# A banded convolution turned round: taps as the stationary operand on 96-token tiles of two token streams, and a transposing DMA to bring the result to channels

## Chip, cores and metric

One core of a Trainium2 chip. The metric is device time in microseconds (us); most executions of one kernel lie within 0.3% of each other. The kernel before takes 400.06 us (median of 3 runs, 399.44 to 400.3).

## The reference, cut to what matters

```python
# x: (8, 4224, 192); weight: (8 heads, 7 taps); w_in: (192, 2*512); A_log: (512,); w_out: (512, 192)
w = softmax(weight, axis=-1)                         # per head, 24 channels a head
xc[b, s, h, g] = sum_k w[h, k] * x[b, s - 6 + k, h, g]    # causal, zeros before each sequence
val, gate = split(xc @ w_in)
h_t = exp(A_log) * h_{t-1} + val_t                   # along each sequence, per inner channel
out = (silu(gate) * h) @ w_out
```

## The kernel before

A step is 1024 tokens of one of the four blocks of 128 inner channels; four steps make a period, 33 periods the loop. The convolution multiplies x (stationary, that is loaded as weights: 128 tokens x 32 padded channels of a head) by a band of taps (moving, that is streamed past them: 134 columns). So its result already has channels on the partitions, as the projections want it. PSUM is the memory that TensorE writes its results to; an eviction is the copy out of it.

```python
ps_c = ctx.enter_context(tc.tile_pool(name="ps_c", bufs=1, space=bass.MemoryType.PSUM))
ps_v = ctx.enter_context(tc.tile_pool(name="ps_v", bufs=2, space=bass.MemoryType.PSUM))
# ... taps: VectorE builds fz, ScalarE's queue writes it to memory and reads the band back
nc.scalar.dma_start(fa, fz.rearrange("p h f -> p (h f)"))
nc.scalar.dma_start(
    tb, dataclasses.replace(fa, offset=FL, ap=[[H * FR - 1, P], [FR, H], [1, W]])
)
# ...
def conv(p):                       # 512 tokens
    pc = ps_c.tile([P, 2, N], FP32, name="pc")
    for b in range(NB):
        for h in range(H):
            q = C32 * (h % HG)
            nc.tensor.matmul(pc[q : q + C32, h // HG, b * P : b * P + w],
                             xb[:, b, h, :], tb[:, h, 0:w], ...)
        # ... at the first block, 8 matmuls of 6 columns for the tokens of the tile before
    nc.scalar.copy(xc, pc)
# ...
def scan(s):                       # one scan of 1024 tokens, cut where a sequence starts
    for lo, hi in zip(ends, ends[1:]):
        nc.vector.tensor_tensor_scan(h[:, lo:hi], av[...], pv[:, lo:hi],
                                     initial=0.0 if lo in cuts else last[c], ...)
# ... loop, per step: scan, gate, output projection of six steps ago,
#     a convolution in every second step, val of the next step, gate, product on GpSimd
```

Of the kernel before, what the change touches and what calls it, by code (L numbers as in the profile page):

```python
# [37 lines left out]
def kernel(  # L38
# [22 lines left out]
    NP = T // N  # L61
    NS = T // N2
    BPB = S // P
    NC = DI // P
    HG = H // 2
    C32 = 32
    assert NS * N2 == T and BPB * P == S and NC == 4 and G <= C32 and HG == 4
    W = P + HALO
    FL = P - 1
# [3 lines left out]
    x4 = xf.rearrange("(n b p) d -> n p b d", b=NB, p=P)  # L73
# [6 lines left out]
    xc_pool = ctx.enter_context(tc.tile_pool(name="xc", bufs=5))  # L80
# [8 lines left out]
    XB = 4  # L89
    raw = {}  # L90

    def load(p):
        t = xraw_pool.tile([P, NB, D], FP32, name="xraw")
        nc.sync.dma_start(t, x4[p])
        raw[p] = t


    FR = FL + W
    ws = singles.tile([P, H, KW], FP32, name="ws")
    nc.sync.dma_start(  # L100
        ws, dataclasses.replace(weight, ap=[[0, P], [KW, H], [1, KW]])
    )
    load(0)
    load(1)


    win = singles.tile([P, 2, D2], BF16, name="win")
    for h in range(H - 1):
        nc.gpsimd.dma_start(  # L109
            win[C32 * (h % HG) : C32 * (h % HG) + C32, h // HG, :],  # L110
            moe_w_in[h * G : h * G + C32, :],
        )
    nc.gpsimd.dma_start(win[96 : 96 + G, 1, :], moe_w_in[(H - 1) * G : H * G, :])
    nc.gpsimd.dma_start(win[96 + G : P, 1, :], moe_w_in[0 : C32 - G, :])  # L114
    xbs = []
    for j in range(XB):
        xb = singles.tile([P, NB, H, C32], BF16, name=f"xb_{j}")
        nc.gpsimd.memset(xb[:, :, :, G:C32], 0.0)
        xbs.append(xb)

    fz = singles.tile([P, H, FR], BF16, name="fz")
# [3 lines left out]
    wmax = singles.tile([P, H], FP32, name="wmax")  # L125
    nc.vector.tensor_reduce(wmax, ws, axis=mybir.AxisListType.X, op=Alu.max)
    nc.vector.tensor_tensor(  # L127
        ws, ws, wmax.unsqueeze(2).to_broadcast([P, H, KW]), op=Alu.subtract
    )
    nc.scalar.activation(ws, ws, Act.Exp)  # L130
    wsum = singles.tile([P, H], FP32, name="wsum")
    nc.vector.tensor_reduce(wsum, ws, axis=mybir.AxisListType.X, op=Alu.add)
    winv = singles.tile([P, H], FP32, name="winv")
    nc.vector.reciprocal(winv, wsum)
    for k in range(KW):
        nc.vector.tensor_tensor(  # L136
            fz[:, :, FL + HALO - k], ws[:, :, k], winv, op=Alu.mult
        )
    f_dram = nc.dram_tensor("taps_scratch", (P, H * FR), BF16, kind="Internal")
    fa = f_dram.ap()  # L140
    nc.scalar.dma_start(fa, fz.rearrange("p h f -> p (h f)"))
    tb = singles.tile([P, H, W], BF16, name="tb")
    nc.scalar.dma_start(
        tb, dataclasses.replace(fa, offset=FL, ap=[[H * FR - 1, P], [FR, H], [1, W]])
# [6 lines left out]
    def cast(p):  # L151
        nc.gpsimd.tensor_copy(  # L152
            xbs[p % XB][:, :, :, 0:G],
            raw.pop(p).rearrange("p b (h g) -> p b h g", g=G),
        )

    cast(0)
    cast(1)
    wout = singles.tile([P, NC, D], BF16, name="wout")
    nc.gpsimd.dma_start(wout, moe_w_out.rearrange("(c p) m -> p c m", p=P))  # L160
    for p in range(2, 6):
        load(p)
    cast(2)
    cast(3)

    xcs = {}

    def conv(p):
        pc = ps_c.tile([P, 2, N], FP32, name="pc")
        xb, xp = xbs[p % XB], xbs[(p - 1) % XB]  # L170
        for b in range(NB):
            begins = (p * NB + b) % BPB == 0
            ends = (p * NB + b + 1) % BPB == 0
            w = P if ends or b == NB - 1 else W
            for h in range(H):
                q = C32 * (h % HG)
                nc.tensor.matmul(  # L177
                    pc[q : q + C32, h // HG, b * P : b * P + w],
                    xb[:, b, h, :],
                    tb[:, h, 0:w],  # L180
                    start=(b == 0), stop=(b == NB - 1), skip_group_check=True,
                )
            if b == 0 and not begins:
                for h in range(H):
                    q = C32 * (h % HG)
                    nc.tensor.matmul(  # L186
                        pc[q : q + C32, h // HG, 0:HALO],
                        xp[:, NB - 1, h, :],
                        tb[:, h, P:W],
                        start=False, stop=False, skip_group_check=True,  # L190
                    )
        xc = xc_pool.tile([P, 2, N], BF16, name="xc")
        nc.scalar.copy(xc, pc)  # L193
        xcs[p] = xc

    def proj(ps, p, m):
        for g in range(2):
            nc.tensor.matmul(  # L198
                ps, win[:, g, m * P : (m + 1) * P], xcs[p][:, g, :],
                start=(g == 0), stop=(g == 1),  # L200
            )
# [3 lines left out]
    def val(s, half):  # L205
        i, c = divmod(s, NC)
        if i >= NS:
            return
        if half == 0:
            pvs[s] = ps_v.tile([P, N2], FP32, name="pv")  # L210
        proj(pvs[s][:, half * N : (half + 1) * N], 2 * i + half, c)
# [3 lines left out]
    def gate(s, half):  # L215
        i, c = divmod(s, NC)
        if half == 0:
            sgs[s] = g_pool.tile([P, N2], BF16, name=f"sg_{c}")
        pg = ps_r.tile([P, N], FP32, name="pr")
        proj(pg, 2 * i + half, NC + c)  # L220
        nc.scalar.activation(sgs[s][:, half * N : (half + 1) * N], pg, Act.Silu)  # L221

    last = [None] * NC
    hs = {}

    def scan(s):
        i, c = divmod(s, NC)
        h = h_pool.tile([P, N2], BF16, name=f"h_{c}")
        pv = pvs.pop(s)
        cuts = [b * P for b in range(2 * NB) if (i * 2 * NB + b) % BPB == 0]  # L230
        ends = sorted(set([0] + cuts + [N2]))
        for lo, hi in zip(ends, ends[1:]):
            nc.vector.tensor_tensor_scan(  # L233
                h[:, lo:hi], av[:, c : c + 1].to_broadcast([P, hi - lo]), pv[:, lo:hi],
                initial=0.0 if lo in cuts else last[c],
                op0=Alu.mult, op1=Alu.add,
            )
            last[c] = h[:, hi - 1 : hi]
        hs[s] = h
# [10 lines left out]
    def outp(v):  # L250
        i, u = divmod(v, NC)
        p = 2 * i + u // 2
# [17 lines left out]
    conv(0)  # L270
    conv(1)
    val(0, 0)
    val(0, 1)
    for s in range(NSTEP + LAG):
        i, c = divmod(s, NC)
        live = s < NSTEP
        if live:
            if c == 0:
                for p in (2 * (i + 3), 2 * (i + 3) + 1):
                    if p < NP:  # L280
                        load(p)
            scan(s)
            if c == DVE_GATE + 1:
                mul(nc.vector, s - 1)
            gate(s, 0)
        if s >= LAG:
            outp(s - LAG)
        if live:
            if c % 2 == 0 and i + 1 < NS:
                conv(2 * (i + 1) + c // 2)  # L290
            val(s + 1, 0)
            gate(s, 1)
            val(s + 1, 1)
            if c != DVE_GATE:
                mul(nc.gpsimd, s)
            else:
                for p in (2 * (i + 2), 2 * (i + 2) + 1):
                    if p < NP:
                        cast(p)
# [30 lines left out]
```

## Time and profile before

| | before |
|---|---|
| time | 400.06 us |
| first projection starts | 26.6 us |
| TensorE, share of the chain that ended last | 89% |
| TensorE, two steps | 5.51 us, of it 0.73 for a convolution of 512 tokens |
| mean granted TensorE clock | 1.00 |
| packets on the DMA queue of SyncE | 69840 |

TensorE has no room in the loop: from the first projection to the last it never waits longer than 0.4 us. The lines are in the prediction, except the first projection:

```profile
26.58 2.19 PE L198 MATMUL pv<-xc,win 128*128 128x512 bf16 x4
```

For the loop, only what shortens TensorE's own work counts; for the start, only what brings the first projection forward.

### The profile page before, as it was taken

What the parts mean: (1) busy time and instruction counts of PE and PEld (TensorE: products, weight loads), DVE (VectorE), ACT (ScalarE), POOL (GpSimd) and SP (SyncE); (2) the same over time, 40 slices, a digit from 0 to 9 for tenths busy, and PEclk for the clock granted to TensorE, in tenths of its full rate; (3) what the DMA queues carried; (4) which work ended last, traced back from release to release, by engine and by line L of the source; (5) the groups of instructions that cost most, each with busy time, mean ns of one, the idle gap of its engine ahead of it and who ended that gap; (6) DMA issues with size and microseconds to landing.
All of it is one profiled execution on the core that took longest, in us unless ns stands there. A gap on an engine that the chain in (4) does not pass through costs nothing.

```text
span 397.6 us, 11114 instructions
## 1 busy us (share of the span) xinstructions
PE 366.6 (92%) x4736; PEld 222.6 (56%) x4736; DVE 332.3 (84%) x205; ACT 287.0 (72%) x466; POOL 268.6 (68%) x183
## 2 busy tenths in 40 slices
PE   0059999999999999999999999999999999999994
PEld 0024556656666566565666656656566565665663
DVE  3009998998899998989999889988899898988890
ACT  1037777777778777777777777777777777777863
POOL 5407877677766776767776667676677666766562
PEclk9999999999999999999999999999999999999999
DMA  5930144555445444455554544445555454441225
GB/s 140 318 96 2 39 135 148 161 161 158 139 142 155 125 126 139 138 160 160 158 150 134 159 132 117 144 129 161 160 160 156 125 157 136 127 140 46 78 79 160
DMA packets 72546, 54.19 MB, mean 136 GB/s; under 512 B 4528, under 2 KB 72112, under 8 KB 72496
## 3 DMA queue, kind: packets, MB, share of 16 engines
q1 hardware_dynamic: 69840, 51.94, 43.5%
q0 software_dynamic: 944, 0.72, 1.1%
q10 hardware_dynamic: 1712, 0.81, 0.7%
q8 instruction: 37, 0.61, 0.7%
q14 instruction: 13, 0.11, 0.1%
HBM read 27.70 MB, written 26.49 MB: 136 GB/s over the span
## 4 chain that ended last, share of the span: by engine, by line
PE 89%; DMA 5%; DVE 2%; ACT 1%; issue 1%; DVEq 1%; POOLq 1%; ACTq 0%
PE pv L198 30%; PE pr L198 28%; PE pr L258 21%; PE pc L177 10%; DMA tb<-taps_scratch 2%; DMA taps_scratch<-fz 2%; DMA ws<-in_weight_dram 1%; DVE h L233 1%; ACT xc L193 1%; DVEq L325 1%; PE pc L186 1%; POOLq L325 1%; DVE y L245 0%; DVE fz L136 0%; ACT sg L221 0%
## 5 line engine op out<-in xcount | busy, mean ns | idle before, releaser
L233 DVE TENSOR_TENSOR_SCAN h<-av,h,pv 128x1024 bf16<-128x1024 f32 (+7 forms) x128 | 270.1, 2112 | 30.3 <-PE pv L198 26.5
L245 POOL TENSOR_TENSOR y<-sg,h 128x1024 bf16<-128x1024 bf16 x99 | 210.9, 2131 | 115.0 <-ACT sg L221 109.6
L221 ACT ACTIVATE sg<-pr 128x512 bf16<-128x512 f32 x264 | 157.7, 597 | 67.0 <-PE pr L198 67.0
L198 PE MATMUL pv<-xc,win 128*128 128x512 bf16 x528 | 158.5, 382 | 0.8 <-DVE h L233 0.6
L198 PE MATMUL pr<-xc,win 128*128 128x512 bf16 x528 | 157.3, 380 | 0.1
L198 PEld LDWEIGHTS <-win 128*128 128x128 bf16 x1056 | 97.2, 98 | 103.0 <-issue 3.0
L258 PE MATMUL pr<-wout,y 128*128 128x192 bf16 x1056 | 108.3, 246 | 1.7 <-POOL y L245 1.7
L258 PEld LDWEIGHTS <-y 128*128 128x128 bf16 x1056 | 91.0, 98 | 32.2 <-POOL y L245 1.9
L193 ACT CAST xc<-pc 128x1024 bf16<-128x1024 f32 x66 | 66.8, 1012 | 17.7 <-PE pc L177 10.6
L177 PE MATMUL pc<-tb,xb 128*32 128x134 bf16 (+1 forms) x2112 | 47.0, 225 | 24.4 <-DMA tb<-taps_scratch 23.3
L265 ACT COPY osb<-pr 128x384 f32<-128x384 f32 x132 | 63.3, 479 | 8.3 <-PE pr L258 2.9
L233 DVE TENSOR_TENSOR_SCAN h<-av,pv 128x1024 bf16<-128x1024 f32 (+7 forms) x32 | 42.5, 1330 | 21.2 <-PE pv L198 21.2
L152 POOL CAST xb<-xraw 128x768 bf16<-128x768 f32 x66 | 52.8, 828 | 2.3 <-DMA xraw<-in_x_dram 2.3
L177 PEld LDWEIGHTS <-xb 128*32 128x32 bf16 x2112 | 32.8, 96 | 35.6 <-issue 23.9
L245 DVE TENSOR_TENSOR y<-sg,h 128x1024 bf16<-128x1024 bf16 x33 | 22.0, 666 | 0.0
L186 PE MATMUL pc<-tb,xb 128*32 128x6 bf16 x512 | 13.1, 167 | 0.0
L186 PEld LDWEIGHTS <-xb 128*32 128x32 bf16 x512 | 10.7, 97 | 0.0
L149 ACT ACTIVATE av<-al 128x4 f32<-128x4 f32 x1 | 0.2, 205 | 8.7 <-DMA taps_scratch<-fz 8.7
L109 POOL DMA_DIRECT2D win<-in_moe_w_in_dram x7 | 3.6, 530 | 0.8 <-POOLq L314 0.8
L130 ACT ACTIVATE ws<-ws 128x56 f32<-128x56 f32 x1 | 0.2, 250 | 4.1 <-DVE ws L127 4.1
L114 POOL DMA_DIRECT2D win<-in_moe_w_in_dram x1 | 0.5, 516 | 3.9 <-DMA win<-in_moe_w_in_dram 3.9
L122 DVE MEMSET fz<- 128x2088 bf16 x1 | 1.8, 1798 | 1.2 <-PEq L314 1.2
(14 smaller groups left out, 6.9 us busy)
## 6 DMA issues: line engine op xcount, KB each, us to landing
xraw<-in_x_dram SPq DMA_DIRECT2D x66, 384.0 KB, 4.7
out_dram<-osb SPq DMA_DIRECT2D x66, 384.0 KB, 2.9
taps_scratch<-fz ACTq DMA_DIRECT2D x1, 522.0 KB, 7.0
win<-in_moe_w_in_dram POOLq DMA_DIRECT2D x7, 64.0 KB, 8.8
tb<-taps_scratch ACTq DMA_DIRECT2D x1, 268.0 KB, 8.2
wout<-in_moe_w_out_dram POOLq DMA_DIRECT2D x1, 192.0 KB, 7.3
win<-in_moe_w_in_dram POOLq DMA_DIRECT2D x1, 48.0 KB, 9.4
ws<-in_weight_dram SPq DMA_DIRECT2D x1, 28.0 KB, 5.3
```

The costliest lines, as they stand in the source:

```text
L109: nc.gpsimd.dma_start(win[C32 * (h % HG) : C32 * (h % HG) + C32, h // HG, :], moe_w_in[h * G : h * G + C32, :],)
L152: nc.gpsimd.tensor_copy(xbs[p % XB][:, :, :, 0:G], raw.pop(p).rearrange("p b (h g) -> p b h g", g=G),)
L177: nc.tensor.matmul(pc[q : q + C32, h // HG, b * P : b * P + w], xb[:, b, h, :], tb[:, h, 0:w], start=(b == 0), stop=(b == NB - 1), skip_gr ...
L186: nc.tensor.matmul(pc[q : q + C32, h // HG, 0:HALO], xp[:, NB - 1, h, :], tb[:, h, P:W], start=False, stop=False, skip_group_check=True,)
L193: nc.scalar.copy(xc, pc)
L198: nc.tensor.matmul(ps, win[:, g, m * P : (m + 1) * P], xcs[p][:, g, :], start=(g == 0), stop=(g == 1),)
L221: nc.scalar.activation(sgs[s][:, half * N : (half + 1) * N], pg, Act.Silu)
L233: nc.vector.tensor_tensor_scan(h[:, lo:hi], av[:, c : c + 1].to_broadcast([P, hi - lo]), pv[:, lo:hi], initial=0.0 if lo in cuts else last[c],
L245: eng.tensor_mul(y, sgs.pop(s), hs.pop(s))
L258: nc.tensor.matmul(po2[:, k, :], ys[NC * i + c][:, t0 : t0 + P], wout[:, c, :], start=(k == 0 and c == 0), stop=(c == NC - 1), skip_group_ ...
L265: nc.scalar.copy(osbs[p][:, b0 : b0 + 2, :], po2)
L325: with _tile.TileContext(nc) as tc:
```

## The change

The intent: make the band of taps the stationary operand (102 tokens x 96), let x stream past, and so replace 2624 small matmuls by 792. (The 102 tokens are 96 and the six before them, the halo, which is zero where a sequence starts.) The result then has tokens on the partitions, and a transposing DMA brings it to channels. 192 channels are 128 + 64; two token streams in lockstep fill one 128-row tile with their two sets of 64. A unit is 192 tokens of each stream; eight units are a group.

```diff
-        t = xraw_pool.tile([P, NB, D], FP32, name="xraw")
-        nc.sync.dma_start(t, x4[p])
+        t = xraw_pool.tile([K, QT, D], FP32, name="xraw")     # K = 96 + 6 = 102
+        if q % QB == 0:                                       # a sequence starts
+            nc.vector.memset(t[0:HALO, 0, :], 0.0)
+            nc.sync.dma_start(t[HALO:K, 0, :], xf[t0 + HALO : t0 + K, :])
+            a0 = 1
+        nc.sync.dma_start(t[:, a0:QT, :], ...)
@@ cast
+        if q + 3 < NQ:
+            load(st, q + 3)                # right after the cast that frees the buffer
@@ conv
-                nc.tensor.matmul(pc[...], xb[:, b, h, :], tb[:, h, 0:w], ...)
+                nc.tensor.matmul(main[:, :, :, lo:e], tb[:, h, :], xu[:, :, :, lo:e], ...)
+                nc.tensor.matmul(mix[:, :, :, b - D1 : hi - D1], tb[:, h, :], xu[:, :, :, b:hi], ...)
-        nc.scalar.copy(xc, pc)
+        nc.scalar.copy(yc[:, :, 2 * kk : 2 * kk + 2, :], pc[0:M, 0 : N + 2 * P]...)
+        if kk == HT // 2 - 1:              # after four units
+            for r in range(3):
+                nc.sync.dma_start_transpose(xcs[g][:, r, ...], yc[:, r, :, :]...)
@@ scan
+        for st in range(2):                # one scan of 512 for each stream
@@ before the loop
-    conv(0)
-    conv(1)
+    for q in range(QT):
+        for st in range(2):
+            cast(st, q)
+        conv(2 * q)
+        conv(2 * q + 1)
(loop order, taps of 102 rows, projection weights in two tiles: cut)
```

More of the change, by code (lines that the diff above doesn't have):

```diff
@@ L60 @@
     T = B * S
-    NP = T // N
-    NS = T // N2
+    TS = T // 2
+    NS = TS // N
     BPB = S // P
     NC = DI // P
-    HG = H // 2
-    C32 = 32
-    assert NS * N2 == T and BPB * P == S and NC == 4 and G <= C32 and HG == 4
-    W = P + HALO
-    FL = P - 1
+    M = 96
+    K = M + HALO
+    QT = 4
+    QB = S // (QT * M)
+    NQ = TS // (QT * M)
+    GT = 16
+    NGR = TS // (GT * M)
+    HT = GT // 2
+    SPG = GT * M // N * NC
+    D1 = P
+    D2R = D - P
+    assert 2 * TS == T and NS * N == TS and BPB * P == S and NC == 4
+    assert QB * QT * M == S and NGR * GT * M == TS and 2 * D2R == P and B % 2 == 0
+    FR = K - 1 + M
     xf = x.rearrange("b s d -> (b s) d")
     of = out.rearrange("b s d -> (b s) d")
-    x4 = xf.rearrange("(n b p) d -> n p b d", b=NB, p=P)
     o4 = of.rearrange("(n b p) d -> n p b d", b=NB, p=P)
@@ L79 @@
     xraw_pool = ctx.enter_context(tc.tile_pool(name="xraw", bufs=6))
-    xc_pool = ctx.enter_context(tc.tile_pool(name="xc", bufs=5))
+    xb_pool = ctx.enter_context(tc.tile_pool(name="xb", bufs=3))
+    yc_pool = ctx.enter_context(tc.tile_pool(name="yc", bufs=2))
+    xc_pool = ctx.enter_context(tc.tile_pool(name="xc", bufs=3))
     h_pool = ctx.enter_context(tc.tile_pool(name="hp", bufs=3))
@@ L87, with load @@
     ps_r = ctx.enter_context(tc.tile_pool(name="ps_r", bufs=2, space=bass.MemoryType.PSUM))
-    XB = 4
     raw = {}
-    def load(p):
-        t = xraw_pool.tile([P, NB, D], FP32, name="xraw")
-        nc.sync.dma_start(t, x4[p])
-        raw[p] = t
-    FR = FL + W
-    ws = singles.tile([P, H, KW], FP32, name="ws")
+    def load(st, q):
+        t = xraw_pool.tile([K, QT, D], FP32, name="xraw")
+        t0 = st * TS + q * QT * M - HALO
+        a0 = 0
+        if q % QB == 0:
+            nc.vector.memset(t[0:HALO, 0, :], 0.0)
+            nc.sync.dma_start(t[HALO:K, 0, :], xf[t0 + HALO : t0 + K, :])
+            a0 = 1
+        nc.sync.dma_start(
+            t[:, a0:QT, :],
+            dataclasses.replace(
+                xf, offset=xf.offset + (t0 + a0 * M) * D,
+                ap=[[D, K], [M * D, QT - a0], [1, D]],
+            ),
+        )
+        raw[st, q] = t
+    ws = singles.tile([K, H, KW], FP32, name="ws")
     nc.sync.dma_start(
-        ws, dataclasses.replace(weight, ap=[[0, P], [KW, H], [1, KW]])
+        ws, dataclasses.replace(weight, ap=[[0, K], [KW, H], [1, KW]])
     )
-    load(0)
-    load(1)
-    win = singles.tile([P, 2, D2], BF16, name="win")
-    for h in range(H - 1):
-        nc.gpsimd.dma_start(
-            win[C32 * (h % HG) : C32 * (h % HG) + C32, h // HG, :],
-            moe_w_in[h * G : h * G + C32, :],
-        )
-    nc.gpsimd.dma_start(win[96 : 96 + G, 1, :], moe_w_in[(H - 1) * G : H * G, :])
-    nc.gpsimd.dma_start(win[96 + G : P, 1, :], moe_w_in[0 : C32 - G, :])
-    xbs = []
-    for j in range(XB):
-        xb = singles.tile([P, NB, H, C32], BF16, name=f"xb_{j}")
-        nc.gpsimd.memset(xb[:, :, :, G:C32], 0.0)
-        xbs.append(xb)
-    fz = singles.tile([P, H, FR], BF16, name="fz")
+    for q in range(3):
+        for st in range(2):
+            load(st, q)
+    w1 = singles.tile([P, D2], BF16, name="w1")
+    nc.gpsimd.dma_start(w1, moe_w_in[0:D1, :])
+    w2 = singles.tile([P, 2, D2], BF16, name="w2")
+    for st in range(2):
+        own, other = (slice(st * D2R, st * D2R + D2R), slice((1 - st) * D2R, (2 - st) * D2R))
+        nc.gpsimd.memset(w2[other, st, :], 0.0)
+        nc.gpsimd.dma_start(w2[own, st, :], moe_w_in[D1:D, :])
+    fz = singles.tile([K, H, FR], BF16, name="fz")
     nc.vector.memset(fz, 0.0)
@@ L124 @@
     nc.scalar.dma_start(al, moe_A_log.rearrange("(c p) -> p c", p=P))
-    wmax = singles.tile([P, H], FP32, name="wmax")
+    wmax = singles.tile([K, H], FP32, name="wmax")
     nc.vector.tensor_reduce(wmax, ws, axis=mybir.AxisListType.X, op=Alu.max)
     nc.vector.tensor_tensor(
-        ws, ws, wmax.unsqueeze(2).to_broadcast([P, H, KW]), op=Alu.subtract
+        ws, ws, wmax.unsqueeze(2).to_broadcast([K, H, KW]), op=Alu.subtract
     )
     nc.scalar.activation(ws, ws, Act.Exp)
-    wsum = singles.tile([P, H], FP32, name="wsum")
+    wsum = singles.tile([K, H], FP32, name="wsum")
     nc.vector.tensor_reduce(wsum, ws, axis=mybir.AxisListType.X, op=Alu.add)
-    winv = singles.tile([P, H], FP32, name="winv")
+    winv = singles.tile([K, H], FP32, name="winv")
     nc.vector.reciprocal(winv, wsum)
     for k in range(KW):
-        nc.vector.tensor_tensor(
-            fz[:, :, FL + HALO - k], ws[:, :, k], winv, op=Alu.mult
-        )
-    f_dram = nc.dram_tensor("taps_scratch", (P, H * FR), BF16, kind="Internal")
+        nc.vector.tensor_tensor(fz[:, :, K - 1 - k], ws[:, :, k], winv, op=Alu.mult)
+    f_dram = nc.dram_tensor("taps_scratch", (K, H * FR), BF16, kind="Internal")
     fa = f_dram.ap()
     nc.scalar.dma_start(fa, fz.rearrange("p h f -> p (h f)"))
-    tb = singles.tile([P, H, W], BF16, name="tb")
+    tb = singles.tile([K, H, M], BF16, name="tb")
     nc.scalar.dma_start(
-        tb, dataclasses.replace(fa, offset=FL, ap=[[H * FR - 1, P], [FR, H], [1, W]])
+        tb, dataclasses.replace(fa, offset=K - 1, ap=[[H * FR - 1, K], [FR, H], [1, M]])
     )
@@ L149, with cast @@
     nc.scalar.activation(av, al, Act.Exp)
-    def cast(p):
+    xbs = {}
+    def cast(st, q):
+        if st == 0:
+            xbs[q] = xb_pool.tile([K, 2, 2, 2, D], BF16, name="xb")
         nc.gpsimd.tensor_copy(
-            xbs[p % XB][:, :, :, 0:G],
-            raw.pop(p).rearrange("p b (h g) -> p b h g", g=G),
-        )
-    cast(0)
-    cast(1)
-    wout = singles.tile([P, NC, D], BF16, name="wout")
-    nc.gpsimd.dma_start(wout, moe_w_out.rearrange("(c p) m -> p c m", p=P))
-    for p in range(2, 6):
-        load(p)
@@ L163 @@
-    cast(2)
-    cast(3)
-    xcs = {}
-    def conv(p):
-        pc = ps_c.tile([P, 2, N], FP32, name="pc")
-        xb, xp = xbs[p % XB], xbs[(p - 1) % XB]
-        for b in range(NB):
-            begins = (p * NB + b) % BPB == 0
-            ends = (p * NB + b + 1) % BPB == 0
-            w = P if ends or b == NB - 1 else W
-            for h in range(H):
-                q = C32 * (h % HG)
+            xbs[q][:, :, st, :, :],
+            raw.pop((st, q)).rearrange("p (j a) d -> p j a d", a=2),
+        )
@@ new lines, in cast, with conv @@
+        if q + 3 < NQ:
+            load(st, q + 3)
+    ycs = {}
+    xcs = {}
+    def conv(u):
+        q, j = divmod(u, 2)
+        g, k = divmod(u, GT // 2)
+        half, kk = divmod(k, HT // 2)
+        xu = xbs[q][:, j, :, :, :]
+        pc = ps_c.tile([P, N2], FP32, name="pc")
+        main = pc[0:M, 0:N].rearrange("p (s a d) -> p s a d", s=2, a=2)
+        mix = pc[0:M, N : N + 2 * P].rearrange("p (a s d) -> p s a d", s=2, a=2)
+        for h in range(H):
+            lo, hi = h * G, h * G + G
+            if lo < D1:
+                e = min(hi, D1)
@@ L177, in conv @@
                 nc.tensor.matmul(
-                    pc[q : q + C32, h // HG, b * P : b * P + w],
-                    xb[:, b, h, :],
-                    tb[:, h, 0:w],
-                    start=(b == 0), stop=(b == NB - 1), skip_group_check=True,
-                )
-            if b == 0 and not begins:
-                for h in range(H):
-                    q = C32 * (h % HG)
-                    nc.tensor.matmul(
-                        pc[q : q + C32, h // HG, 0:HALO],
-                        xp[:, NB - 1, h, :],
-                        tb[:, h, P:W],
-                        start=False, stop=False, skip_group_check=True,
-                    )
@@ L192, in conv @@
-        xc = xc_pool.tile([P, 2, N], BF16, name="xc")
-        nc.scalar.copy(xc, pc)
-        xcs[p] = xc
-    def proj(ps, p, m):
-        for g in range(2):
-            nc.tensor.matmul(
-                ps, win[:, g, m * P : (m + 1) * P], xcs[p][:, g, :],
-                start=(g == 0), stop=(g == 1),
-            )
+                    main[:, :, :, lo:e], tb[:, h, :], xu[:, :, :, lo:e],
+                    start=(h == 0), stop=(e == D1), skip_group_check=True,
+                )
+            if hi > D1:
+                b = max(lo, D1)
+                nc.tensor.matmul(
+                    mix[:, :, :, b - D1 : hi - D1], tb[:, h, :], xu[:, :, :, b:hi],
+                    start=(b == D1), stop=(hi == D), skip_group_check=True,
+                )
@@ new lines, in conv @@
+        if kk == 0:
+            ycs[g, half] = yc_pool.tile([M, 3, HT, P], BF16, name="yc")
+        yc = ycs[g, half]
+        nc.scalar.copy(
+            yc[:, :, 2 * kk : 2 * kk + 2, :],
+            pc[0:M, 0 : N + 2 * P].rearrange("p (r a d) -> p r a d", r=3, a=2),
+        )
+        if kk == HT // 2 - 1:
+            if half == 0:
+                xcs[g] = xc_pool.tile([P, 3, GT * M], BF16, name="xc")
+            for r in range(3):
+                nc.sync.dma_start_transpose(
+                    xcs[g][:, r, half * HT * M : (half + 1) * HT * M].rearrange(
+                        "p (t m) -> p t m", m=M
+                    ),
+                    yc[:, r, :, :].rearrange("p t d -> p (t d)"),
+                )
+            ycs.pop((g, half))
@@ L203, with proj @@
+    def proj(ps, i, st, m):
+        g, k = divmod(i, GT * M // N)
+        t = slice(k * N, k * N + N)
+        cols = slice(m * P, m * P + P)
+        nc.tensor.matmul(ps, w1[:, cols], xcs[g][:, st, t], start=True, stop=False)
+        nc.tensor.matmul(ps, w2[:, st, cols], xcs[g][:, 2, t], start=False, stop=True)
     pvs = {}
@@ L210, in val @@
             pvs[s] = ps_v.tile([P, N2], FP32, name="pv")
-        proj(pvs[s][:, half * N : (half + 1) * N], 2 * i + half, c)
+        proj(pvs[s][:, half * N : (half + 1) * N], i, half, c)
     sgs = {}
@@ L219, in gate @@
         pg = ps_r.tile([P, N], FP32, name="pr")
-        proj(pg, 2 * i + half, NC + c)
+        proj(pg, i, half, NC + c)
         nc.scalar.activation(sgs[s][:, half * N : (half + 1) * N], pg, Act.Silu)
-    last = [None] * NC
+    last = {}
     hs = {}
@@ L229, in scan @@
         pv = pvs.pop(s)
-        cuts = [b * P for b in range(2 * NB) if (i * 2 * NB + b) % BPB == 0]
-        ends = sorted(set([0] + cuts + [N2]))
-        for lo, hi in zip(ends, ends[1:]):
-            nc.vector.tensor_tensor_scan(
-                h[:, lo:hi], av[:, c : c + 1].to_broadcast([P, hi - lo]), pv[:, lo:hi],
-                initial=0.0 if lo in cuts else last[c],
-                op0=Alu.mult, op1=Alu.add,
-            )
-            last[c] = h[:, hi - 1 : hi]
+        cuts = [b * P for b in range(NB) if (i * NB + b) % BPB == 0]
+        ends = sorted(set([0] + cuts + [N]))
+        for st in range(2):
+            for lo, hi in zip(ends, ends[1:]):
+                o = st * N
+                nc.vector.tensor_tensor_scan(
+                    h[:, o + lo : o + hi],
+                    av[:, c : c + 1].to_broadcast([P, hi - lo]),
+                    pv[:, o + lo : o + hi],
+                    initial=0.0 if lo in cuts else last[st, c],
+                    op0=Alu.mult, op1=Alu.add,
+                )
+                last[st, c] = h[:, o + hi - 1 : o + hi]
         hs[s] = h
@@ L251, in outp @@
         i, u = divmod(v, NC)
-        p = 2 * i + u // 2
+        p = (u // 2) * NS + i
         po = ps_r.tile([P, N], FP32, name="pr")
@@ L269 @@
     NSTEP = NS * NC
-    conv(0)
-    conv(1)
+    UNITS = {0: 0, 1: 1, 3: 2, 4: 3, 6: 4, 7: 5, 9: 6, 10: 7}
+    CASTS = {9: (0, 4), 10: (1, 4), 0: (0, 1), 1: (1, 1), 3: (0, 2), 4: (1, 2), 6: (0, 3), 7: (1, 3)}
+    for q in range(QT):
+        for st in range(2):
+            cast(st, q)
+        conv(2 * q)
+        conv(2 * q + 1)
+    for st in range(2):
+        cast(st, QT)
+    wout = singles.tile([P, NC, D], BF16, name="wout")
+    nc.gpsimd.dma_start(wout, moe_w_out.rearrange("(c p) m -> p c m", p=P))
     val(0, 0)
@@ L275 @@
         i, c = divmod(s, NC)
+        gr, o = divmod(s, SPG)
         live = s < NSTEP
         if live:
-            if c == 0:
-                for p in (2 * (i + 3), 2 * (i + 3) + 1):
-                    if p < NP:
-                        load(p)
+            if o in CASTS:
+                st, dq = CASTS[o]
+                q = QT * (gr + 1) + dq
+                if q < NQ:
+                    cast(st, q)
             scan(s)
@@ L288 @@
         if live:
-            if c % 2 == 0 and i + 1 < NS:
-                conv(2 * (i + 1) + c // 2)
+            if o in UNITS and gr + 1 < NGR:
+                conv((GT // 2) * (gr + 1) + UNITS[o])
             val(s + 1, 0)
@@ L295 @@
                 mul(nc.gpsimd, s)
-            else:
-                for p in (2 * (i + 2), 2 * (i + 2) + 1):
-                    if p < NP:
-                        cast(p)
 _INS = ['x', 'weight', 'moe_w_in', 'moe_A_log', 'moe_w_out']
```

## The prediction

> **What bounds the kernel now.** I read the busy shares first, then the chain of waits, then the timeline of a steady stretch, then the start, and last the DMA queues.
>
> ```profile
> PE 366.6 (92%) x4736; PEld 222.6 (56%) x4736; DVE 332.3 (84%) x205; ACT 287.0 (72%) x466; POOL 268.6 (68%) x183
> PE 89%; DMA 5%; DVE 2%; ACT 1%; issue 1%; DVEq 1%; POOLq 1%; ACTq 0%
> ```
>
> The chain lies on TensorE for 89% of the span. A busy TensorE need not be full, so I look at how far apart its matmuls start. The timeline of TensorE, over about one pair of steps (start, length, both in us):
>
> ```profile
> 200.07 0.82 PE L258 MATMUL pr<-wout,y 128*128 128x192 bf16 x8
> 200.73 0.59 PE L198 MATMUL pv<-xc,win 128*128 128x512 bf16 x2
> ...
> 202.46 0.82 PE L258 MATMUL pr<-wout,y 128*128 128x192 bf16 x8
> 203.21 0.30 PE L177 MATMUL pc<-tb,xb 128*32 128x134 bf16 x8
> ...
> 203.39 0.52 PE L177 MATMUL pc<-tb,xb 128*32 128x134 bf16 x24
> 203.84 0.60 PE L198 MATMUL pv<-xc,win 128*128 128x512 bf16 x2
> ...
> 205.58 0.82 PE L258 MATMUL pr<-wout,y 128*128 128x192 bf16 x8
> ```
>
> From output projection to output projection with a convolution between: 205.58 - 200.07 = 5.51 us, two steps of 2.755 us. In it a pair of 512-column matmuls starts every 0.433 us (0.216 each) and eight 192-column ones take 0.66 us (0.082 each). So two steps need 8 x 0.433 + 2 x 0.66 = 4.78 us without convolution, 2.392 a step; the convolution of 512 tokens, with its gaps, is the remaining 0.73 us (0.63 of it from 203.21 to 203.84). TensorE is really full: 132 steps x 2.755 = 364 us. Only the 0.73 us can be saved.
>
> VectorE is second. Its scans, from the timeline and from the groups by form:
>
> ```profile
> 38.63 6.80 DVE L233 TENSOR_TENSOR_SCAN h<-av,h,pv 128x1024 bf16<-128x1024 f32 x3
> 45.35 0.67 DVE L245 TENSOR_TENSOR y<-sg,h 128x1024 bf16<-128x1024 bf16 x1
> L233 DVE TENSOR_TENSOR_SCAN h<-av,h,pv 128x512 bf16<-128x512 f32 x4 | 5.1, 1280 | 0.9 <-PE pv L198 0.8
> ```
>
> Three scans of 1024 occupy 45.35 - 38.63 = 6.72 us, so 2.24 each start to start, although one lasts 2.35: neighbours overlap by about 0.1. With a quarter of a 0.67 multiply (about 0.15 after overlap) VectorE needs 2.39 us a step against TensorE's 2.755.
>
> The start, in the chain of waits:
>
> ```profile
> 15.12 8.16 DMA tb<-taps_scratch
> 23.33 1.10 PE pc L177 x24
> 24.45 1.02 ACT xc L193
> 25.96 0.71 PE pc L177 x18
> 26.69 1.02 ACT xc L193
> 27.76 1.01 PE pv L198 x2
> ```
>
> The band of taps comes at 23.3 us; two convolutions alternate with their evictions through the single PSUM buffer; the projections begin at 26.6 and the first scan at 28.9. The DMA queues:
>
> ```profile
> q1 hardware_dynamic: 69840, 51.94, 43.5%
> xraw<-in_x_dram SPq DMA_DIRECT2D x66, 384.0 KB, 4.7
> ```
>
> 69840 packets took 43.5% of 16 engines' 397.6 us: 39.6 ns for a packet of some 744 B.
>
> **What the Trainium skill says.** "TensorE: Matmul & The Clock Gate", section "Back-to-back issue gap": in a stream of weight load and matmul pairs both set the spacing, about 81 ns at 128 columns, where the matmul alone would take 56. The trace agrees as far as it goes: 82 ns a pair, but at 192 columns, where the matmul needs about that anyway. The same page, section "Weight-path perf modes", says the fast weight load is on only with 128 weights; section "LDWEIGHTS" gives columns / 1.2 ns[...], which is 80 ns for 96 columns. The trace has no 96-column load; it records 98 ns for both 32 and 128 columns, so its duration says nothing of the rate. "DMA: Bandwidth & Descriptors", section "Why a DMA increments its semaphore by 16 and not by 1", says a transfer is spread over the largest number of engines up to 16 that divides the outer dimensions: 102 partitions give 6, against 16 for the 128 of now. No 102-partition load is in this trace. Its section "Latency and other measured facts" gives 261 GB/s for a transposing DMA that is not contiguous; no transpose is in this trace either.
>
> **The change, part by part.**
>
> *Convolution on TensorE.* Removed: 66 convolutions of 512 tokens, 2624 matmuls, four of 32 columns side by side. Added: 88 units of 384 tokens (192 of each stream), each nine matmuls with a 102x96 weight: six over the first 128 channels and three over the other 64, with 96 moving columns mostly and 768 in sum. Cost of a unit, c: streaming 768 columns at 0.216/512 = 0.42 ns gives 0.32 us, the least it can be. If weight loads limit it, nine x 80 ns = 0.72 us (estimate from the skill's formula). Taking pairs at about 65 ns between the two, c = 0.6 us. A loop step now holds 2/3 of a unit, not half an old convolution. With a 0.1 us gap, break-even is 2/3 x (c + 0.1) = 0.363, c = 0.445. Eight units move ahead of the loop, so loop work is 132 x 2.392 + 80 x (c + 0.1): 315.7 + 56 = 372 us at c = 0.6. Before it is 315.7 + 64 x 0.73 = 362. That is +10 us; at c = 0.35 it would be -10, at c = 0.72 +19.
>
> *Scans.* Each step has two scans of 512 (one per stream) in place of one of 1024. By the difference of forms, an element costs (2.345 - 1.280)/512 = 2.08 ns, so a 512 scan back to back takes 2.24 - 1.07 = 1.17 us, a pair 2.34, a step 2.34 + 0.15 = 2.49 us. VectorE gains about 0.1 us x 132 = 13 us of work but stays below TensorE. On the path: nothing, unless c is at its least, where a step would be 2.69.
>
> *ScalarE and GpSimd.* The eviction of a unit is 768 wide: from 1012 ns for 1024 and 479 for 384, about 0.80 us; 88 x 0.80 = 70 us against 66.8. GpSimd casts 88 tiles of 768 elements at 0.83 = 73 us against 52.8, so 289 us. Both stay off the path.
>
> *Transposes.* 66 of 96x1024 bf16, 0.2 MB each. The instruction order shows that the first half of a group is wanted seven steps after its last unit, the second half five: 5 x 2.8 = 14 us for an eviction and three transposes. At 261 GB/s the three move in 2.3 us (estimate); even at several us each they are hidden in the loop.
>
> *Start.* Eight units now precede the first projection, each conv, eviction, conv through the same single PSUM buffer: 0.6 (more while the clock is cold) + 0.8 + about 0.25 of latency = 1.65 us, eight of them 13 us. The taps come over 6 engines beside the x loads on the same 6, so I put them a little later, 24.5 us. Half of the transposes finish meanwhile. The first projection begins at about 38 us instead of 26.6: +11 us. The drain (388.6 to 397.6) is the same.
>
> Sum: 400 + 11 (start) + 10 (loop) = 421 us. I put 418 as the middle, because the first rival below has about a third of the weight and lies lower.
>
> **The rivals.** (1) *The weight loads hide completely.* Then c is 0.35 to 0.4, the loop is 6 to 10 us shorter and the result is 400 to 405: the longer start eats the gain. For it: 128-column loads hide today behind 80 ns matmuls. Against: 96-column matmuls of 40 ns hide only half as much. (2) *The DMA engines become the bound.* On six engines an x load is 68 packets each; 88 x 68 x 39.6 ns = 237 us, plus stores 66 x 32 x 39.6 = 84, plus transposes 13 MB / 16 engines at the skill's rate, about 50 us: 371 us on each of those six, 90 to 95% of the span. If transposes are twice as slow, loads and transposes arrive late and the loop follows them: 430 to 460 us. Against: loads are issued nine steps ahead. (3) *VectorE takes over.* If the 512 scans do not overlap, a pair costs 2.56 and a step 2.73: with c small this sets 132 x 2.75, again near today's loop, about 410. The overlap seen argues against.
>
> **Range and chances.** To be faster by 2% (under 392) takes c near its streaming floor and almost none of the longer start; four in a hundred. Under 408 takes c below about 0.45, one in five. The upper side is c = 0.72 (428) and some DMA lateness: 450. So 402 to 450 with 418 in the middle.
>
> **What would show it.** The eight conv and eviction pairs alone between the arrival of the taps and the first projection, ending near 38 us, prove the start. The time between the first matmul of a unit and the next projection gives c: 0.6 expected, 0.35 refutes the weight-load limit. Step length: 2.392 + 2/3 x 0.7 = 2.86 us. VectorE waits for projections in every step if TensorE bounds; if scans lie back to back, rival 3 is right. Waits of projections on the transposed tile, or of casts on x, inside the loop, show rival 2; then the prediction is too low. A start no longer than now and c under 0.4 would make it too high.

## The result, and the profile after

The changed kernel takes 417.98 us (median of 4 runs, 417.73 to 418.21) against 399.88 of before in the same rounds: ratio 1.0453, 95% interval 1.0434 to 1.0471. Ratios here are the mean time of one kernel's runs over that of the other's of the same rounds, so not quite the ratio of the medians quoted. Executions over 1.5% slower than the fastest of the same kernel are left out of the means. The total hit the forecast of 418; its parts did not, as the next views show.

The page of the changed kernel: busy times, the chain, the queue of SyncE (packets, MB, share of 16 engines).

```profile
PE 361.8 (87%) x2860; PEld 232.9 (56%) x2904; DVE 339.4 (82%) x341; ACT 286.7 (69%) x488; POOL 286.0 (69%) x197
PE 74%; DMA 8%; DVE 6%; issue 4%; POOL 2%; ACT 2%; SPq 2%; POOLq 1%; DVEq 0%; ACTq 0%
q1 hardware_dynamic: 124268, 66.50, 69.9%
```

TensorE's share of the chain fell from 89 to 74%: the kernel waits where it did not.

A steady stretch, timeline of TensorE and its weight loads (PEld):

```profile
201.14 0.82 PE L286 MATMUL pr<-wout,y 128*128 128x192 bf16 x8
...
201.72 0.39 PEld L191 LDWEIGHTS <-tb 102*96 102x96 bf16 x6
201.80 0.41 PE L191 MATMUL pc<-xb,tb 102*96 102x96 bf16 x6
...
202.05 0.31 PE L197 MATMUL pc<-xb,tb 102*96 102x64 bf16 x3
...
202.20 0.38 PE L224 MATMUL pv<-xc,w 128*128 128x512 bf16 x1
```

From a unit's first matmul to the next projection is 202.20 - 201.80 = 0.40 us, nine pairs at 0.044 us, with no gap beside it. The predicted unit was 0.6 us and 0.1 of gap. So where nothing waits, the loop became shorter, not longer.

The start, from the timeline:

```profile
24.86 0.67 PE L191 MATMUL pc<-xb,tb 102*96 102x96 bf16 x6 [24.86 <-DMA tb<-taps_scratch]
...
26.70 0.59 PE L191 MATMUL pc<-xb,tb 102*96 102x96 bf16 x6 [0.88 <-ACT yc L204]
...
37.51 0.59 PE L191 MATMUL pc<-xb,tb 102*96 102x96 bf16 x6 [0.88 <-ACT yc L204]
...
38.20 0.63 PE L224 MATMUL pv<-xc,w 128*128 128x512 bf16 x1
```

The eight units start 1.75 to 1.85 us apart, each waiting for ScalarE to empty the one buffer; the first projection comes at 38.2 us, 11.6 after that of before.

What TensorE's projections waited for in the changed kernel (us in total, times, longest):

```profile
PE pv L224 <- DVE h L259: 9.8, 4, 3.0
PE pv L225 <- DMA xc<-yc: 2.6, 3, 1.2
PE pv L224 <- DMA xc<-yc: 1.5, 1, 1.5
```

Four waits for a scan, 9.8 us, and four for a transpose, 4.1 us (0.4 of them before the loop). The kernel before had no such wait above 0.4 us. One of the four, in the timelines of VectorE, GpSimd and TensorE:

```profile
252.29 0.22 DVE L107 MEMSET xraw<- 6x192 f32 x1 [2.84 <-POOL xb L169]
252.44 2.32 DVE L259 TENSOR_TENSOR_SCAN h<-av,h,pv 128x512 bf16<-128x512 f32 x2
257.88 0.22 DVE L107 MEMSET xraw<- 6x192 f32 x1 [3.12 <-POOL xb L169]
```
```profile
254.91 2.12 POOL L273 TENSOR_TENSOR y<-sg,h 128x1024 bf16<-128x1024 bf16 x1 [2.71 <-DVE h L259]
256.97 0.82 POOL L169 CAST xb<-xraw 102x768 bf16<-102x768 f32 x1
```
```profile
260.40 0.38 PE L224 MATMUL pv<-xc,w 128*128 128x512 bf16 x1 [3.04 <-DVE h L259]
...
261.52 0.63 PE L225 MATMUL pv<-xc,w 128*128 128x512 bf16 x1
261.94 0.63 PE L224 MATMUL pr<-xc,w 128*128 128x512 bf16 x1
```

Where a sequence starts, VectorE zeroes six halo rows of a new x tile. The zeroing lasts 0.22 us, but it stands in VectorE's queue ahead of the scan, and must wait until GpSimd's cast has freed that tile. The cast stands behind a product of 2.1 us, which itself waits for the scan of the step before. So scan, product, cast, zeroing and next scan run one after the other, and TensorE waits 3.0 us. Shortly after, matmuls of 512 columns start 0.42 us apart (261.52 to 261.94) in place of 0.216, so at half rate. In this trace such a stretch follows both waits of 3.0 us and neither of the two of 1.8 us; in the trace of e2 it also follows two waits of 1.8 us, so the runs give no rule. The zeroing occurs at three places (two streams each), near 68 to 71, 157 to 163 and 252 to 258 us; TensorE waited after four of these six. The mean granted clock is 0.987.

### The profile page after: what moved, and what is told of

It is laid out like the page before. It is cut to its first block, busy times and chain, and to the rows that moved or that the text cites. A ratio compares the mean times of both kernels' runs of the same rounds, so it can differ in the third digit from the quotient of the medians.

```text
span 416.0 us, 7730 instructions
## 1 busy us (share of the span) xinstructions
PE 361.8 (87%) x2860; PEld 232.9 (56%) x2904; DVE 339.4 (82%) x341; ACT 286.7 (69%) x488; POOL 286.0 (69%) x197
## 4 chain that ended last, share of the span: by engine, by line
PE 74%; DMA 8%; DVE 6%; issue 4%; POOL 2%; ACT 2%; SPq 2%; POOLq 1%; DVEq 0%; ACTq 0%
PE pr L286 18%; PE pr L224 13%; PE pv L224 13%; PE pr L225 12%; PE pv L225 11%; DVE h L259 5%; PE pc L191 5%; DMA xc<-yc 3%; PE pc L197 3%; DMA tb<-taps_scratch 3%; DMA taps_scratch<-fz 2%; SPq L212 2%; POOL y L273 2%; DMA ws<-in_weight_dram 1%; ACT yc L204 1%
## 5 line engine op out<-in xcount | busy, mean ns | idle before, releaser
L259 DVE TENSOR_TENSOR_SCAN h<-av,h,pv 128x512 bf16<-128x512 f32 (+3 forms) x256 | 296.8, 1211 | 14.4 <-PE pv L225 9.5
L273 POOL TENSOR_TENSOR y<-sg,h 128x1024 bf16<-128x1024 bf16 x99 | 214.6, 2168 | 91.5 <-ACT sg L245 52.4
L224 PE MATMUL pv<-xc,w 128*128 128x512 bf16 x264 | 101.6, 385 | 12.1 <-DVE h L259 9.8
L224 PE MATMUL pr<-xc,w 128*128 128x512 bf16 x264 | 101.0, 383 | 1.9 <-issue 0.2
L225 PE MATMUL pr<-xc,w 128*128 128x512 bf16 x251 | 96.1, 383 | 0.0
L169 POOL CAST xb<-xraw 102x768 bf16<-102x768 f32 x88 | 71.8, 822 | 29.1 <-DMA xraw<-in_x_dram 27.3
L225 PE MATMUL pv<-xc,w 128*128 128x512 bf16 x233 | 89.4, 384 | 2.6 <-DMA xc<-yc 2.6
L225 PEld LDWEIGHTS <-w 128*128 128x128 bf16 x528 | 52.1, 99 | 59.2 <-issue 13.0
L204 ACT CAST yc<-pc 96x768 bf16<-96x768 f32 x88 | 70.0, 795 | 18.5 <-PE pc L197 18.5
L224 PEld LDWEIGHTS <-w 128*128 128x128 bf16 x528 | 52.1, 99 | 52.9 <-issue 5.2
L191 PE MATMUL pc<-xb,tb 102*96 102x96 bf16 x528 | 38.0, 211 | 31.0 <-DMA tb<-taps_scratch 24.9
L191 PEld LDWEIGHTS <-tb 102*96 102x96 bf16 x528 | 36.7, 132 | 33.0 <-DMA tb<-taps_scratch 24.9
L259 DVE TENSOR_TENSOR_SCAN h<-av,pv 128x512 bf16<-128x512 f32 (+3 forms) x32 | 25.1, 799 | 34.4 <-remote 33.5
L197 PE MATMUL pc<-xb,tb 102*96 102x96 bf16 (+1 forms) x264 | 28.9, 221 | 0.0
L197 PEld LDWEIGHTS <-tb 102*96 102x96 bf16 x264 | 20.3, 133 | 0.0
(17 smaller groups left out, 10.6 us busy)
```

What stands on the lines that cost most here:

```text
L169: nc.gpsimd.tensor_copy(xbs[q][:, :, st, :, :], raw.pop((st, q)).rearrange("p (j a) d -> p j a d", a=2),)
L191: nc.tensor.matmul(main[:, :, :, lo:e], tb[:, h, :], xu[:, :, :, lo:e], start=(h == 0), stop=(e == D1), skip_group_check=True,)
L197: nc.tensor.matmul(mix[:, :, :, b - D1 : hi - D1], tb[:, h, :], xu[:, :, :, b:hi], start=(b == D1), stop=(hi == D), skip_group_check=True,)
L204: nc.scalar.copy(yc[:, :, 2 * kk : 2 * kk + 2, :], pc[0:M, 0 : N + 2 * P].rearrange("p (r a d) -> p r a d", r=3, a=2),)
L224: nc.tensor.matmul(ps, w1[:, cols], xcs[g][:, st, t], start=True, stop=False)
L225: nc.tensor.matmul(ps, w2[:, st, cols], xcs[g][:, 2, t], start=False, stop=True)
```

## The experiments

My theory after the two traces: the changed loop is faster by itself, and four separate losses hide it, namely the longer start, the zeroing on VectorE, late transposes on crowded DMA engines, and late taps. The main rival: the DMA queues bound the loop, and whatever wait is removed returns elsewhere. All kernels gave a correct result.

**e1: the zeroing on GpSimd.**

```diff
-            nc.vector.memset(t[0:HALO, 0, :], 0.0)
+            nc.gpsimd.memset(t[0:HALO, 0, :], 0.0)
```

> One edit to the changed kernel: the zeroing of the halo at a sequence start moves from VectorE to GpSimd, which also makes the cast that it waits for. Theory (the zeroing holds the scans up, and the scans the projections, 9.75 us of TensorE idle before projections that wait for a scan): 408 us, within 2, and no such TensorE wait over 1 us. Rival (the DMA queues pace the loop, so a stall removed is waited for elsewhere): 415 us or more.

Measured 409.61 us, ratio to before 1.0243 (1.0214 to 1.0272): 8.4 us less than the changed kernel. No projection waits for a scan any more. The waits for transposes, however, grew from 4.1 to 6.4 us:

```profile
PE pv L225 <- DMA xc<-yc: 3.3, 5, 1.1
PE pv L224 <- DMA xc<-yc: 3.1, 1, 3.1
```

The theory holds. The rival gets little support: 4.2 us of these waits lie at 50.8 and 52.4 us (2.6 us at the same place in the changed kernel), before the first of the removed pauses, at 71 us, so the edit did not cause them by ending pauses. New, at 119.5, 152.2 and 184.8 us, are three waits of 1.5 us together, where a loop without the pauses may have run into the DMA.

**e2: 112 partitions in place of 102 for x tiles and taps.** The ten further rows are loaded and not used.

```diff
+    KL = 112
-        t = xraw_pool.tile([K, QT, D], FP32, name="xraw")
+        t = xraw_pool.tile([KL, QT, D], FP32, name="xraw")
-                ap=[[D, K], [M * D, QT - a0], [1, D]],
+                ap=[[D, kl], [M * D, QT - a0], [1, D]],    # kl = 112, but 102 at the very end
(the same for ws, fz, tb and the taps in memory; matmuls and casts still use 102 rows)
```

> One edit: x tiles, taps and their scratch get 112 partitions in place of 102 (the ten extra rows are never used), so that 16 divides the count. Theory (102 rows use only 6 of 16 DMA engines, and these six make the taps and the transposes late): taps land 2 to 4 us sooner, the 3.8 us of TensorE waits for transposes inside the loop fall to under 1, time 410 to 413 us. Rival (the number of engines does not matter, the transposes themselves are slow): 416 to 420 us, as ten per cent more bytes are loaded.

Measured 412.78 us, ratio 1.031 (1.0264 to 1.0357), though 9% more of x is loaded. The taps came at 21.8 us instead of 24.9, and the waits for transposes in the loop were gone:

```profile
14.19 10.62 DMA tb<-taps_scratch
13.22 8.54 DMA tb<-taps_scratch
```

(start and length, first the changed kernel, then e2.) Both predicted signs are there. The profile is of the fastest of the four runs, 409.02 us; the others took 412.7 to 413.2.

**e3: the units before the loop in two buffers.**

```diff
-        pc = ps_c.tile([P, N2], FP32, name="pc")
+        pc = ps_v.tile([P, N2], FP32, name="pv") if early else ps_c.tile([P, N2], FP32, name="pc")
```

> One edit: the eight convolution units before the loop use the two idle buffers of the projections' PSUM pool in turn, so that a unit need not wait for the eviction of the one before. Theory (the chain of convolution, eviction, convolution costs the start, but the first transposes land just behind it): first projection 2 to 3 us sooner, 415 us. Rival (the chain alone sets the start): 6 us sooner, 411 to 412 us.

Measured 416.47 us, ratio 1.0428 (1.0396 to 1.0461). This interval overlaps that of the changed kernel, so a gain of 1.5 us is not clear of noise; what the run shows is where the waits went. The units hardly waited any more for evictions (0.5 us in all, 6.2 in the changed kernel), but the projections then waited for transposes, from the timeline of TensorE:

```profile
35.15 0.58 PE L224 MATMUL pv<-xc,w 128*128 128x512 bf16 x1 [2.70 <-DMA xc<-yc]
...
49.20 0.61 PE L224 MATMUL pv<-xc,w 128*128 128x512 bf16 x1 [2.51 <-DMA xc<-yc]
```

The first projection is 3 us earlier, and the next transposes are then late by 2.5. The chain of evictions was not alone in setting the start.

**e4: the three edits together**, and every second eviction of the start on VectorE.

> The three edits together, and every second eviction of the start on VectorE. Theory (four separate losses that add): 418 minus 10 minus 6 minus 4 = 398 us, within 3. Rival (the losses hide one another, or the DMA engines bound the loop): 404 us or more.

Measured 395.22 us, ratio 0.9893 (0.985 to 0.9937). The three alone take off 8.4 + 5.2 + 1.5 = 15.1 us, together they take off 22.8. So the losses do not simply add. That they covered one another is an explanation that e3 supports, where the time won from evictions was waited for at transposes; but the extra eviction on VectorE is in the sum too, and no run separates it.

**e5: taps ahead of the x loads**, on top of e4.

```diff
-    for q in range(3):
+    for q in range(2):
         for st in range(2):
             load(st, q)
-    nc.scalar.dma_start(fa, ...)
-    nc.scalar.dma_start(tb, ...)
+    nc.sync.dma_start(fa, ...)
+    nc.sync.dma_start(tb, ...)
+    for st in range(2):
+        load(st, 2)
```

> The three edits of the last run of before, and the taps go out and come back on SyncE's queue ahead of the third pair of x loads (they went on ScalarE's queue beside all six). Theory (the x loads slow the taps down at the start): taps land 1 to 3 us sooner than the 22.1 us of the run with all three edits, time 392 to 394 us. Rival (the round trip through memory is latency, not bandwidth): the same 395 us, or later if SyncE's order delays it.

Measured 388.84 us, ratio 0.973 (0.9716 to 0.9745), better than expected. The chain of waits of e5, start and length:

```profile
6.16 7.21 DMA taps_scratch<-fz
13.39 2.62 DMA tb<-taps_scratch
16.06 0.67 PE pv L195 x6
```

Fetching the band takes 2.62 us here; it took 10.6 in the changed kernel and 9.0 in e4. So most of that time was queueing and not a fixed latency. The run changes the queue and the order at once, and which of the two did it is not separated. The first projection now comes at 25.6 us; in e4 it came at 31.7.

**e6: every unit's matmuls twice**, on top of e4 (the second set overwrites the first, so the result is the same).

```diff
-        for h in range(H):
-            ...
+        for _ in range(2):
+            for h in range(H):
+                ...
```

> The run with all three edits, with every convolution unit's nine matmuls issued twice into the same place (result the same). Measures c where TensorE sets the pace. If a unit costs 0.40 us, as the trace of the change has it (201.80 to 202.20): 395 plus 80 times 0.40 in the loop and up to 8 times 0.4 before it, so 427 to 431 us. If it cost the predicted 0.6 us: 443 us or more.

Measured 428.12 us, 32.9 more than e4. Over the 80 units in the loop that is 0.41 us a unit, over all 88 it is 0.37. The unit's price at the end of the span is the 0.40 us of the trace, not 0.6.

**e7: the kernel before with split scans.**

```diff
-        ends = sorted(set([0] + cuts + [N2]))
+        ends = sorted(set([0] + cuts + [N, N2]))
```

> The kernel before, with every scan of 1024 split into two of 512 (the second starts from the first one's end). Theory (VectorE has 0.3 us a step to spare, so the split costs nothing): 400 us, within 2. Rival (the split is a part of the loss, 0.1 to 0.2 us a step): 410 us or more.

Measured 401.41 us, ratio 1.0041 (1.0026 to 1.0056). The split is nearly free while TensorE bounds the loop. This is what the prediction said of it.

**e8 and e9: every transpose twice**, the second into a spare tile. e8 does it to the changed kernel (x loads of 102 rows), e9 to e4 (112 rows).

```diff
+            for r in range(3):
+                xd = xd_pool.tile([P, HT, M], BF16, name="xd")
+                nc.sync.dma_start_transpose(xd, yc[:, r, :, :].rearrange("p t d -> p (t d)"))
```

> The changed kernel with every transpose done a second time into a spare tile. Theory (the six DMA engines that carry the x loads are nearly full: 88 x 68 packets of 39.6 ns are 237 us, the stores 84 us, and the transposes, from the packets' share of the queues, some 118 us, 439 us together): with 118 us more the DMA queue sets the time, 500 to 560 us. Rival (only latency was short, the engines have room): 418 to 430 us.

> The run with all three edits (x loads on all 16 DMA engines), with every transpose done twice, to set beside the changed kernel with transposes twice (487 us, 69 more than without). Theory (what filled up there were the six engines that carry the x loads): spread over 16 the doubling costs much less, 395 to 425 us. Rival (the transposes' own rate or SyncE's issue is the limit, whatever the loads do): again about 65 us more, 460 us or above.

Measured: e8 487.11 us (ratio 1.2174), 69 us more than without the doubling; e9 399.38 us (ratio 1.0002), 4 us more than e4. The same extra work is nearly free on top of e4, whose loads have 112 rows. But e4 differs from the changed kernel in its other two edits as well; transposes doubled with the 112 rows alone were not run. In e8 the overload shows at the output: ScalarE's copies to the output tile waited 62.1 us for stores (26 times, at most 5.3), against 1.8 us in e9.

```profile
ACT osb L297 <- DMA out_dram<-osb: 62.1, 26, 5.3
```

For e8 the expectation of 500 to 560 was too high, and so was my price of a transpose packet. The queue lines of e4 and e9 give it, and that of e8 beside the changed kernel's a second time:

```profile
q1 hardware_dynamic: 128558, 69.12, 72.4%
```
```profile
q1 hardware_dynamic: 181358, 82.11, 91.5%
```
```profile
q1 hardware_dynamic: 177068, 79.49, 75.6%
```

0.915 x 16 x 396.6 - 0.724 x 16 x 394.5 = 1236 us for 52800 packets, 23.4 ns each; 0.756 x 16 x 485.8 - 0.699 x 16 x 416.0 = 1224 us for as many, 23.2 each. A kernel's 66 transposes are then 3300 x 23.4 = 77 us on each of 16 engines if they spread evenly, not 118. On the six engines that the loads would use, that makes 237 + 84 + 77 = 398 us in the changed kernel, of a span of 416, and 475 in e8, which took 487. This is an estimate, and a rough one: it takes 39.6 ns for the other packets from the kernel before, while the changed kernel's own line leaves (0.699 x 16 x 416.0 - 1236) / 71468 = 47.8 ns for them, with which the sum would be 464 and exceed the span. So the account makes near-full engines likely and does not say how full they were. No view shows single DMA engines, so "six" rests on the section of the Trainium skill that the prediction cites ("DMA: Bandwidth & Descriptors", "Why a DMA increments its semaphore by 16 and not by 1") and on e2, e8 and e9 together, not on a count.

**e10: the kernel before with its taps on SyncE's queue**, ahead of its third to sixth x load. The control for e5.

```diff
-    nc.scalar.dma_start(fa, ...)
-    nc.scalar.dma_start(tb, ...)
+    nc.sync.dma_start(fa, ...)
+    nc.sync.dma_start(tb, ...)
```

> The kernel before, with its two tap transfers moved to SyncE's queue ahead of the third to sixth x loads, as in the run that reached 388.8 us. Theory (the better start is not a gain of the changed convolution and can be had without it): 6 to 7 us sooner, 393 to 395 us. Rival (the taps of before were not slowed by the x loads): 400 us.

Measured 395.3 us, ratio 0.9885 (0.987 to 0.99). A start improved in this way gives 4.6 us to the old design too, less than the 6 to 7 expected. So of the 2.7% of e5 some 1.2% are not due to the new convolution; 0.973 / 0.9885 = 0.984, the other 1.6%, are the new convolution together with the repairs to its own losses.

**e11: projection weights fetched later**, on top of e5 (the three weight transfers follow the second pair of casts).

```diff
     for q in range(QT):
         for st in range(2):
             cast(st, q)
+        if q == 1:
+            fetch_w()
```

> The run that reached 388.8 us, with the projection weights fetched after the second pair of casts in place of at the very start. Theory (the scratch write of the taps, 7.2 us for 0.34 MB, shares the DMA engines with 1 MB of weights): taps 2 to 3 us sooner and time 386 to 387 us. Rival (the weights then come too late or the write is latency): 389 us or more.

Measured 387.62 us, ratio 0.9697 (0.9677 to 0.9717), the fastest kernel here. The scratch write fell from 7.2 to 3.5 us, but the first projection came only 0.9 us earlier (24.7), since the chain now passes through an x load of 9.4 us. Against e5, timed in other rounds, the intervals just touch: a gain of some 0.3% that is not clear, and short of the 386 to 387 us expected. Whether later weights help the kernel before was not tried.

## Why the prediction was right or wrong, point by point

The time and the direction were right, but the total was luck: the loop's own work was put 25 us too high, and losses of some 22 us that the prediction does not have made up for it. Its chances do not agree with each other either: it gives the first rival (400 to 405 us) a third of the weight and all times under 408 us a fifth. Two small slips change nothing: the weight loads read as 98 ns are 96 for 32 columns and 98 for 128, and in the third rival 2.56 + 0.15 is 2.71, not 2.73.

- **Start, +11 us: right, and for its reason.** Measured +11.6. Taps at 24.9 (24.5 predicted), 1.75 to 1.85 us a unit (1.65 predicted). It named queueing on fewer engines as why the taps are late; e2 and e5 bear this out. It did not see that the transposes stand right behind this chain (e3).
- **Convolution in the loop, +10 us: wrong. This is the step that failed, "Taking pairs at about 65 ns between the two, c = 0.6 us".** A pair costs 44 ns and a unit 0.40 us without a gap (the trace and e6), so the 80 units in the loop cost 32 us where the old convolution took 64 x 0.73 = 47: a gain of 15 us, not a loss of 10. The first rival, which said this, was right on c and wrong on the total.
- **Zeroing on VectorE: not in the prediction at all.** "On the path: nothing" counted VectorE's work and not its order. An instruction of 0.22 us that waits for another engine in front of a scan cost 9.8 us of TensorE's time, and e1 gives back 8.4 us in total.
- **Transposes, "hidden in the loop": nearly right.** Four waits, 4.1 us in all. The second rival was right that the engines are near full, as far as the rough account goes (398 of 416 us, 371 in the prediction), and wrong on the consequence, as the loop did not follow them until the transposes were doubled.
- **Scans, GpSimd and ScalarE: right.** e7 costs 0.4%. The evictions were predicted at 70 us and took 70.0, GpSimd at 289 and took 286.
- **The drain, "the same": wrong by 2.5 us.** From the end of the last projection to the end of the span it was some 10.2 us and is 12.7; the last 29 matmuls took 4.24 us after a pause of 2.4, and 2.68 before after one of 1.7.

Added up: 11.6 (start) - 15 (convolution) + 9.8 (scans late) + 3.8 (transposes in the loop) + 2.5 (drain) = 12.7 of the 18.4 us by which the span grew. Of the remaining 6 us the trace places some 3 in the two stretches at half rate: from 165.85 to 169.22 us eight matmuls of 512 columns took 3.37 us, where 8 x 0.216 = 1.73; from 261.26 to 264.80 four of them, eight of 192 columns and a unit took 3.54, where 0.86 + 0.66 + 0.40 = 1.92. The last 3 us or so are not placed, and no run separates these stretches from the pauses before them.

## What to carry to other kernels

Before trusting an engine's spare time, look at what stands in its queue ahead of the work on the path, and what that instruction waits for: a tiny fill behind another engine's buffer release can stop a loop. When a tile gets a number of partitions that 16 does not divide (102 here), ask what it does to the spread of its DMA. When a redesign loses, repair its side losses one by one and together, and give the old kernel the repairs that it could use as well, before judging the idea.

## What the Trainium skill lacked or had wrong

- "TensorE: Matmul & The Clock Gate", section "LDWEIGHTS": columns / 1.2 gives 80 ns for a 96-column weight load, and the section names no mode for it. Here pairs of a 96-column load and a matmul of at most 96 columns follow each other every 44 ns, although each load's record lasts 132 ns. Which mode the loads used isn't shown.
- The same page, section "Back-to-back issue gap": it gives the spacing in a stream of pairs for 128 and 512 columns only, 81 and 131 ns. For pairs of 96 and 64 columns the runs show 44 ns (0.40 us for nine), and the 131 ns does not fit: pairs of 512 columns start every 216 ns in both kernels.
- "DMA: Bandwidth & Descriptors", section "Latency and other measured facts", and "Advanced Engine Details and Errata", section "X-Bar Transpose (TRN2)": 261 GB/s where not contiguous, and transposes as fast as regular DMAs. Here 66 transposes of 96x1024 bf16 (13.0 MB) take 77 us of each of 16 engines if they spread evenly, about 168 GB/s beside other traffic: 23.4 ns a packet of 246 bytes on average, where a packet of some 744 bytes took 39.6 ns in the kernel before.
- The section "Why a DMA increments its semaphore by 16 and not by 1" of that DMA page fits the runs (6 engines for 102 rows, 16 for 112, though no view counts them), but no page says what it is worth: 5.2 us in e2, and 69 against 4 us for doubled transposes in e8 and e9, which differ in two more edits.
- No page gives the time that SyncE spends on issuing a transposing DMA of this shape: a median of 1.30 us in e2, at least 1.21.
